# First expert phase entered by token tiles, with the next routing's setup behind it

## The chip, the core and the metric

One core of a Trainium2 chip runs the whole kernel. The metric is device time in microseconds, the median of several runs; lower is better. Engines are named as in the profile: PE (matmul), PEld (its weight loads), DVE (vector), ACT (activation), POOL (issues the indirect DMAs here), SP (issues the others).

## The reference

Local-and-global attention makes 4352 tokens (8 batches of 544) of width 512, and a router with capacity gives each token to one of eight experts, 544 tokens to each. The greedy walk in order of logits is what the routing has to reproduce; each expert is two matrix products with a ReLU.

```python
logits = x @ w_gate                      # N = 4352, E = 8, cap = 544
order = np.argsort(-flat)                # all (token, expert) pairs
for idx in order:
    tok, e = (int(idx) // E, int(idx) % E)
    if assigned[tok] >= 0 or counts[e] >= cap:
        continue
    assigned[tok] = e
    counts[e] += 1
...
for e in range(E):
    mask = assigned == e
    h = np.maximum(x[mask] @ w1[e], 0.0)   # 512 -> 1024
    out[mask] = h @ w2[e]                  # 1024 -> 512
```

## The kernel before

Attention fills roughly the first 230 us of the span, the first routing follows, and then come eight expert phases, one for each expert in the order in which the experts fill up.

**Precision.** Every product in a phase is made of three matmuls on rounded numbers: high by high, high by low, low by high. So each operand has a high part, which ACT rounds (`xh`, `w1h`, `w2h`, `hh`), and a low part, which DVE makes by subtracting (`xl`, `w1l`, `w2l`, `hl`).

**A phase** (`ffn`) has two halves on PE. In the H half, for each f (8 slices of 128 hidden units) and each half hf of the 544 tokens (272 columns, the slice q), a group of 12 matmuls (4 slices of the width, 3 products each; line 849) fills a PSUM tile `H` with three buffers. ACT writes `hh` from it, and DVE's `hl` is not issued at once: it is put into the list `fill` and issued at the end of the next group or when the planner sees a pause (`bubble`). After a short fp32 part (line 867) the Y half multiplies by w2, four token tiles of 24 matmuls each (line 877).

**Tokens** arrive as five tiles `xg` of 128, 128, 128, 128 and 32 rows, gathered by indirect DMA (`load_x`). `trans_x` transposes a tile on PE into an `H` buffer (line 724), ACT writes `xh` (line 726), DVE writes `xl`; those DVE rows carry the line of the wrapper `Queue`, 405.

**Routing** of the next expert runs beside a phase. `rt.setup` is ten DVE instructions (`r_m` to `r_oh`) that make `r_G` and `r_oh`; `search` has eight turns, each with 18 small matmuls `R` on PE (line 468) that read `r_G` and `r_oh`, a product `r_ce` on DVE, two more matmuls, then a scan and a new `r_G` on DVE; the rest of `phase` makes `widx` (addresses of the weights) and `idx` (addresses of the tokens).

**Order.** Every engine works through its instructions in the order in which this program issues them. A planner written into the kernel sets that order: `V.now` is its estimate of PE's time, `V.busy` its estimate of DVE's, booked by `Queue` as 130 ns and 1.05 or 0.55 ns for each element. After each matmul `step` adds to `V.now`, may issue one waiting item of `todo` (low parts of weights, transposes of the next phase, output), and lets the routing go on once `V.now` has passed the time that it asked for, which is `V.busy + HOP` before each group of its matmuls.

**The entry to the first phase** (lines 890 to 914) is written out by hand: first routing, gathers of x and w2, some idle matmuls (`HEAT`), the setup of the next routing, the low parts of the first halves of w1 (`split_w1`, line 702 in the trace), the transposes of all five tiles, and then `V.now = V.busy` and the phases.

Of the kernel before, what the change touches and what calls it, by code (L numbers as in the profile page):

```python
# [8 lines left out]
F32 = mybir.dt.float32  # L9
# [3 lines left out]
AF = mybir.ActivationFunctionType  # L13
ALU = mybir.AluOpType
# [4 lines left out]
B, H, SL, SG, D = 8, 8, 512, 32, 64  # L19
# [645 lines left out]
def experts(ctx, tc, A, xd, ident, rt, out):  # L665
    nc = tc.nc
    wp = ctx.enter_context(tc.tile_pool(name="wp", bufs=1))
    st = ctx.enter_context(tc.tile_pool(name="st", bufs=2))
    ps = ctx.enter_context(tc.tile_pool(name="fps", bufs=1, space=PSUM))
    w1h = [wp.tile([128, FF], F32R, name=f"w1h{c}") for c in range(4)]  # L670
    w1l = [wp.tile([128, FF], F32R, name=f"w1l{c}") for c in range(4)]
# [3 lines left out]
    xh = wp.tile([128, 4, CAP], F32R, name="xh")  # L675
    xl = wp.tile([128, 4, CAP], F32R, name="xl")
    hh = wp.tile([128, 8, CAP], F32R, name="hh")
    hl = wp.tile([128, 8, CAP], F32R, name="hl")
    h32 = wp.tile([128, 8, 32], F32, name="h32")
    part = [wp.tile([128, DM], F32R, name=f"part{k}") for k in range(2)]  # L680
    sizes = [128, 128, 128, 128, 32]
    HF = CAP // 2
# [5 lines left out]
    def load_w1(ph):  # L688
        raws = []
        for k in range(2):  # L690
            raw = st.tile([128, 2, FF], F32, name="w1r", bufs=2)
            gather(raw.rearrange("p a b -> p (a b)"), A["w1"], k * E * 128 * 2 * FF, rt.widx[ph][:, :1])
            raws.append(raw)
        return raws
# [5 lines left out]
    def split(hi, lo, raw, eng):  # L700
        nc.scalar.activation(hi, raw, AF.Copy)  # L701
        eng.tensor_tensor(lo, raw, hi, op=ALU.subtract)

    def split_w1(raws, j, eng):
        q = slice(512 * (j % 2), 512 * (j % 2) + 512)
        split(w1h[j // 2][:, q], w1l[j // 2][:, q], raws[j // 4][:, (j // 2) % 2, q], eng)
# [13 lines left out]
    def trans_x(xg, t):  # L720
        n = sizes[t]
        p = ps.tile([128, 4, 128], F32, name="H", bufs=3)
        for d in range(4):
            nc.tensor.transpose(p[:, d, :n], xg[t][:n, 128 * d:128 * d + 128], ident[:n, :n])  # L724
        q = slice(128 * t, 128 * t + n)
        nc.scalar.activation(xh[:, :, q], p[:, :, :n], AF.Copy)
        V.tensor_tensor(xl[:, :, q], p[:, :, :n], xh[:, :, q], op=ALU.subtract)
# [6 lines left out]
    V = rt.V  # L734
    V.now = V.busy = 0.0
    pool, dma, need = [0.0], [0.0], [0.0]
    fill, todo, raw1 = [], [], {}
# [20 lines left out]
    def bubble():  # L758
        while fill:
            fill.pop(0)()  # L760

    def at(tag, t, f, cond=None):
        todo.append((tag, t, cond, f))

    def pending(*tags):
        return any(x[0] in tags for x in todo)

    def force(tag, n=9):
        while pending(tag) and n:
            todo.pop([x[0] for x in todo].index(tag))[3]()  # L770
            n -= 1

    def step(ns):
        V.now += ns
        for i, (tag, t, cond, f) in enumerate(todo):
            if t <= V.now and (cond is None or cond()):
                todo.pop(i)
                f()
                break
        while not done[0] and V.now >= need[0]:  # L780
            v = next(routing, None)
            if v is None:
                done[0] = True
            elif v < 0:
                bubble()
            else:
                need[0] = v
        if V.busy < V.now and (done[0] or need[0] > V.now + SLACK):
            bubble()
# [7 lines left out]
    def get_w1(p, half):  # L797
        raw1[p] = load_w1(p)
        r = [pool_op(1040, 1 << 20) for _ in range(2)]
        for i in range(4):  # L800
            at(f"a{p}", r[i // 2], lambda j=2 * i: low1(p, j), lambda: (half or mid[0] == p - 1) and calm())
        for i in range(4):
            at(f"b{p}", r[i // 2], lambda j=2 * i + 1: low1(p, j), lambda: mid[0] == p - 1 and calm())

    def get_x(p):
        xg = load_x(p)
        for t in range(5):
            r = pool_op(1040, sizes[t] * 2048)
            at(f"x{p}", r, lambda t=t: trans_x(xg, t), lambda: mid[0] == p - 1)

    def get_w2(p):
        load_w2(p)
        r = [pool_op(1040, 1 << 20) for _ in range(2)]
        for j in range(8):
            at(f"w{p}", r[j // 4], lambda j=j: low2(j), lambda: cur[0] == p and calm())

    def out_tile(ph, t, p):
        n = sizes[t]
        while len([x for x in todo if x[0] == "out"]) > 3:
            force("out", 1)  # L820
        y = st.tile([128, DM], F32, name="y", bufs=4)
        nc.scalar.activation(y[:n], p[:n], AF.Copy)  # L822

        def put():
            scatter(ph, t, y)
            wrote[0] = pool_op(1040, n * 2048) + LAND
        at("out", V.now + 900, put, lambda: V.now >= wrote[0])

    def ffn(ph):
        nxt = ph + 1  # L830
        t0 = V.now
        cur[0] = ph
        half = []
        if nxt < E:
            at(f"g{nxt}", t0, lambda: get_w1(nxt, half), lambda: nxt in rt.widx and not pending(f"b{ph}"))
            at(f"h{nxt}", t0, lambda: get_x(nxt), lambda: nxt in rt.idx and (mid[0] == ph or V.now > t0 + TX))
            at(f"v{nxt}", t0, lambda: get_w2(nxt), lambda: mid[0] == ph and nxt in rt.widx and
               (not pending(f"h{nxt}") or V.now > t0 + TW))
        for f in range(8):
            if f == 4:  # L840
                force(f"b{ph}")
                half.append(True)
            for hf in range(2):
                q = slice(HF * hf, HF * hf + HF)
                p = ps.tile([128, HF], F32, name="H", bufs=3)
                fs = slice(128 * f, 128 * f + 128)
                for d in range(4):
                    for k, (w, x) in enumerate(((w1h, xh), (w1h, xl), (w1l, xh))):
                        nc.tensor.matmul(p, w[d][:, fs], x[:, d, q], start=(d + k == 0), stop=(d + k == 5))  # L849
                        step(117)  # L850
                nc.scalar.activation(hh[:, f, q], p, AF.Relu)  # L851
                if hf:
                    nc.scalar.activation(h32[:, f], p[:, HF - 32:HF], AF.Relu)  # L853
                while fill:
                    fill.pop(0)()
                fill.append(lambda p=p, f=f, q=q: V.scalar_tensor_tensor(
                    hl[:, f, q], p, 0.0, hh[:, f, q], op0=ALU.max, op1=ALU.subtract))

        while fill:
            fill.pop(0)()  # L860
        force(f"w{ph}")

        p = ps.tile([128, DM], F32, name="Y", bufs=3)
        for i in range(2):
            for c in range(4):
                f = 2 * c + i
                nc.tensor.matmul(p[32 * c:32 * c + 32], h32[:, f], w2r[f // 4][:, f % 4], start=(i == 0), stop=(i == 1))  # L867
            step(930)
        mid[0] = ph
        nc.scalar.activation(part[0], p, AF.Copy)  # L870
        V.tensor_tensor(part[1], p, part[0], op=ALU.subtract)
        for t in range(4):
            p = ps.tile([128, DM], F32, name="Y", bufs=3)
            for f in range(8):
                q = slice(128 * t, 128 * t + 128)
                for k, (h, w) in enumerate(((hh, w2h), (hh, w2l), (hl, w2h))):
                    nc.tensor.matmul(p, h[:, f, q], w[f], start=(f + k == 0), stop=(f + k == 9))  # L877
                    step(216)
            out_tile(ph, t, p)
            if t == 0:  # L880
                p = ps.tile([128, DM], F32, name="Y", bufs=3)
                for k in range(2):
                    nc.tensor.matmul(p[:32], rt.eye4, part[k], start=(k == 0), stop=(k == 1))
                    step(216)
                out_tile(ph, 4, p)
        while nxt < E and (pending(f"g{nxt}", f"h{nxt}", f"a{nxt}", f"x{nxt}", f"v{nxt}") or nxt not in raw1):
            step(120)
            bubble()

    raws = None  # L890
# [3 lines left out]
    for _ in rt.phase(0):  # L894
        if raws is None and 0 in rt.widx:
            raws = load_w1(0)
    xg = load_x(0)
    load_w2(0)
    for _ in range(HEAT):
        nc.tensor.matmul(heat[:, :128], ident, ident, start=True, stop=True)  # L900
    raw1[0] = raws
    for _ in rt.setup(slice(0, 34)):
        pass
    for j in range(4):
        split_w1(raws, 2 * j, nc.vector)
    for t in range(5):
        trans_x(xg, t)
    V.now = V.busy
    for j in range(4):
        at("b0", 0, lambda j=j: low1(0, 2 * j + 1), calm)  # L910
    for j in range(8):
        at("w0", 0, lambda j=j: low2(j), calm)
    for ph in range(E):
        ffn(ph)
    force("out")


# [75 lines left out]
```

## Time and profile before

| | us |
|---|---|
| median of 3 runs | 772.55 (771.23 to 774.29) |
| profiled execution | 769.7 |
| its span, first to last instruction | 767.9 |
| mean granted PE clock | 0.971 |
| PE busy in the span | 708.8 |
| DVE busy in the span | 506.8 |

Times within the profile count from the span's first instruction. A row of the timeline gives start, length, engine, line, operation, what it writes and reads, and in brackets how long the engine was idle before it and what ended that. A row of busy time by stretch gives the stretch, its length, then busy time and count of instructions for PE, PEld, DVE, ACT and POOL, the granted clock, the DMA engines' share and GB/s.

### The profile page before, as it was taken

What the parts mean: (1) busy time and instruction counts of PE and PEld (TensorE: products, weight loads), DVE (VectorE), ACT (ScalarE), POOL (GpSimd) and SP (SyncE); (2) the same over time, 40 slices, a digit from 0 to 9 for tenths busy, and PEclk for the clock granted to TensorE, in tenths of its full rate; (3) what the DMA queues carried; (4) which work ended last, traced back from release to release, by engine and by line L of the source; (5) the groups of instructions that cost most, each with busy time, mean ns of one, the idle gap of its engine ahead of it and who ended that gap; (6) DMA issues with size and microseconds to landing.
All of it is one profiled execution on the core that took longest, in us unless ns stands there. A gap on an engine that the chain in (4) does not pass through costs nothing.

```text
span 767.9 us, 21120 instructions
## 1 busy us (share of the span) xinstructions
PE 708.8 (92%) x8636; PEld 568.8 (74%) x8636; DVE 506.8 (66%) x1829; ACT 313.1 (41%) x849; POOL 162.2 (21%) x190
## 2 busy tenths in 40 slices
PE   8999999999994489999998999999998999999993
PEld 7667777777762378789688778778777877988972
DVE  6788787777786777677577667677666766641400
ACT  4656666666650143244144134224323414542310
POOL 5221111111000220240231151043024015312011
PEclk9999999999997579999999999999999999999998
DMA  9999879878501340440250081072044018531000
GB/s 353 404 359 341 329 278 332 281 300 321 195 20 56 124 154 2 180 146 13 107 202 28 9 287 43 1 256 82 1 167 156 15 38 286 175 117 59 1 32 27
DMA packets 32415, 120.50 MB, mean 157 GB/s; under 512 B 6720, under 2 KB 6976, under 8 KB 24128
## 3 DMA queue, kind: packets, MB, share of 16 engines
q1 hardware_dynamic: 22080, 67.78, 23.8%
q0 software_dynamic: 10240, 51.39, 18.9%
q8 instruction: 68, 1.11, 0.6%
q14 instruction: 27, 0.22, 0.1%
HBM read 101.32 MB, written 17.83 MB: 155 GB/s over the span
## 4 chain that ended last, share of the span: by engine, by line
PE 47%; DVE 7%; DMA 3%; issue 3%; ACT 3%; POOL 0%; POOLq 0%; ACTq 0%; DVEq 0%
PE Y L877 20%; PE H L849 18%; PE R L468 5%; DMA xg<-xd,idx 2%; PE Y L867 2%; DVE w2l L405 2%; PE H L724 2%; DVE r_G L405 1%; ACT w2h L701 1%; DMA w1r<-in_w_dram,widx 1%; DVE hl L405 1%; DVE w1l L405 1%; DVE r_pm L405 1%; ACT w1h L701 0%; DVE xl L405 0%
## 5 line engine op out<-in xcount | busy, mean ns | idle before, releaser
L849 PE MATMUL H<-xh,w1h 128*128 128x272 f32 x512 | 152.8, 298 | 12.7 <-DVE hl L405 10.7
L849 PE MATMUL H<-xh,w1l 128*128 128x272 f32 x512 | 150.6, 294 | 0.0
L849 PE MATMUL H<-xl,w1h 128*128 128x272 f32 x512 | 149.9, 293 | 0.0
L849 PEld LDWEIGHTS H<-xh,w1h 128*128 128x128 f32 x512 | 97.3, 190 | 17.8 <-DVE hl L405 8.7
L145 ACT ACTIVATE p<-p,nm 128x128 f32<-128x128 f32 x256 | 81.8, 392 | 65.8 <-DVE ls L165 33.7
L851 ACT ACTIVATE hh<-H 128x272 fp32r<-128x272 f32 x128 | 51.0, 398 | 138.6 <-PE H L849 138.4
L877 PE MATMUL Y<-w2h,hh 128*128 128x512 f32 x256 | 103.3, 403 | 0.0
L877 PE MATMUL Y<-w2h,hl 128*128 128x512 f32 x256 | 102.8, 401 | 0.0
L877 PE MATMUL Y<-w2l,hh 128*128 128x512 f32 x256 | 102.6, 401 | 0.0
L849 PEld LDWEIGHTS H<-xl,w1h 128*128 128x128 f32 x512 | 97.6, 191 | 0.0
L849 PEld LDWEIGHTS H<-xh,w1l 128*128 128x128 f32 x512 | 97.4, 190 | 0.0
L134 PE MATMUL S<-qk,qz 128*64 128x128 f32 x1024 | 70.7, 280 | 4.4 <-DVE qz L86 1.8
L685 POOL DMA_INDIRECT w1r<-in_w_dram,widx x16 | 16.2, 1013 | 268.0 <-DVE r_a L405 160.9
L822 ACT ACTIVATE y<-Y 128x512 f32<-128x512 f32 (+1 forms) x40 | 23.5, 594 | 120.8 <-PE Y L877 102.0
L405 DVE SCALAR_TENSOR_TENSOR hl<-H,hh 128x272 fp32r<-128x272 f32 x128 | 53.6, 434 | 25.9 <-ACT h L853 15.3
L86 POOL COPY qz<-q 64x544 f32<-64x544 f32 x60 | 38.7, 645 | 146.2 <-DMA q<-in_qk_dram 104.2
L134 PEld LDWEIGHTS S<-qk,qz 128*64 128x64 f32 x1024 | 55.3, 138 | 16.8 <-issue 9.7
L405 DVE TENSOR_TENSOR w2l<-w2r,w2h 128x512 fp32r<-128x512 f32 x64 | 42.7, 689 | 37.2 <-ACT w2h L701 36.7
L731 POOL DMA_INDIRECT out_dram<-y,idx x40 | 41.8, 1045 | 116.9 <-ACT y L822 57.3
L141 DVE CUSTOM_DVE_ANT_0 p<-S,mask 128x128 f32<-128x128 f32 x256 | 58.8, 285 | 6.1 <-PE S L134 4.4
L877 PEld LDWEIGHTS Y<-w2h,hh 128*128 128x128 f32 x256 | 48.2, 188 | 16.0 <-issue 5.9
L701 ACT ACTIVATE w1h<-w1r 128x512 fp32r<-128x512 f32 x64 | 36.7, 623 | 46.4 <-DMA w1r<-in_w_dram,widx 46.2
(164 smaller groups left out, 1213.7 us busy)
## 6 DMA issues: line engine op xcount, KB each, us to landing
vw<-in_vw_dram SPq DMA_DIRECT2D x32, 1040.0 KB, 7.9
qk<-in_qk_dram SPq DMA_DIRECT2D x32, 432.0 KB, 5.5
q<-in_qk_dram SPq DMA_DIRECT2D x32, 272.0 KB, 5.4
xd<-xs SPq DMA_DIRECT2D x8, 1024.0 KB, 6.4
xd<-xg SPq DMA_DIRECT2D x64, 8.0 KB, 5.2
xg<-xd,idx POOLq DMA_INDIRECT x40, 3.7
out_dram<-y,idx POOLq DMA_INDIRECT x40, 2.8
mask<-in_mask_dram SPq DMA_DIRECT2D x1, 512.0 KB, 5.5
```

What stands on the lines that cost most here:

```text
L86: eng.tensor_copy(z[r, :, h, :], q[r].rearrange("p (j i) -> p j i", i=32))
L134: nc.tensor.matmul(st[64 * r:64 * r + 64, c, :], z[:, j].rearrange("p h i -> p (h i)"), kw[:, k0:k0 + 128], start=True, stop=True)
L141: nc.vector.tensor_tensor_reduce(s.p[:, c, :], st[:, c, :], mask[:, 4 * s.u + c, :], 1.0, -BIG, ALU.add, ALU.max, nm[:, c:c + 1])
L145: nc.scalar.activation(s.p[:, c, :], s.p[:, c, :], AF.Exp, bias=nm[:, c:c + 1], scale=SCALE)
L405: return op(*args, **kw)
L468: s.nc.tensor.matmul(out, *args, **kw)
L701: nc.scalar.activation(hi, raw, AF.Copy)
L731: nc.gpsimd.indirect_dma_start(out=out, out_offset=bass.IndirectOffsetOnAxis(ap=rt.idx[ph][:n, t:t + 1], axis=0), in_=y[:n], in_offset=None)
L822: nc.scalar.activation(y[:n], p[:n], AF.Copy)
L849: nc.tensor.matmul(p, w[d][:, fs], x[:, d, q], start=(d + k == 0), stop=(d + k == 5))
L851: nc.scalar.activation(hh[:, f, q], p, AF.Relu)
L877: nc.tensor.matmul(p, h[:, f, q], w[f], start=(f + k == 0), stop=(f + k == 9))
```

## The change

At the entry, the low parts of w1 come first, then the transposes of three tiles, then the setup; in the first phase alone the groups begin with (f, hf) = (0, 0), (1, 0), and tiles 3 and 4 are transposed in front of (0, 1), which is followed by (1, 1) and the usual order. The two loops over f and hf become one; for the other phases they run as they did.

```diff
-    def ffn(ph):
+    def ffn(ph, late=None):
...
-        for f in range(8):
-            if f == 4:
+        groups = [(f, hf) for f in range(8) for hf in range(2)]
+        if late:
+            groups[:4] = (0, 0), (1, 0), (0, 1), (1, 1)
+        for f, hf in groups:
+            if (f, hf) == (4, 0):
                 force(f"b{ph}")
                 half.append(True)
-            for hf in range(2):
...
+            if (f, hf) == (0, 1) and late:
+                late()
...
     raw1[0] = raws
+    for j in range(4):
+        split_w1(raws, 2 * j, nc.vector)
+    for t in range(3):
+        trans_x(xg, t)
     for _ in rt.setup(slice(0, 34)):
         pass
-    for j in range(4):
-        split_w1(raws, 2 * j, nc.vector)
-    for t in range(5):
-        trans_x(xg, t)
     V.now = V.busy
...
     for ph in range(E):
-        ffn(ph)
+        ffn(ph, (lambda: [trans_x(xg, t) for t in (3, 4)]) if ph == 0 else None)
```

More of the change, by code (lines that the diff above doesn't have):

```diff
@@ L838, in ffn @@
                (not pending(f"h{nxt}") or V.now > t0 + TW))
-        for f in range(8):
-            if f == 4:
+        groups = [(f, hf) for f in range(8) for hf in range(2)]
[3 more added lines that the diff above has]
+            if (f, hf) == (4, 0):
                 force(f"b{ph}")
                 half.append(True)
-            for hf in range(2):
[L844 to L857, printed above, removed]
+            if (f, hf) == (0, 1) and late:
+                late()
+            q = slice(HF * hf, HF * hf + HF)
+            p = ps.tile([128, HF], F32, name="H", bufs=3)
+            fs = slice(128 * f, 128 * f + 128)
+            for d in range(4):
+                for k, (w, x) in enumerate(((w1h, xh), (w1h, xl), (w1l, xh))):
+                    nc.tensor.matmul(p, w[d][:, fs], x[:, d, q], start=(d + k == 0), stop=(d + k == 5))
+                    step(117)
+            nc.scalar.activation(hh[:, f, q], p, AF.Relu)
+            if hf:
+                nc.scalar.activation(h32[:, f], p[:, HF - 32:HF], AF.Relu)
+            while fill:
+                fill.pop(0)()
+            fill.append(lambda p=p, f=f, q=q: V.scalar_tensor_tensor(
+                hl[:, f, q], p, 0.0, hh[:, f, q], op0=ALU.max, op1=ALU.subtract))
         while fill:
```

## The prediction

> **What bounds the kernel now.** I read the page's first two parts, then the timeline around the seam between attention and the first expert phase, then busy time by half phase, then the chain and the waits at the next seams.
>
> ```profile
> PE 708.8 (92%) x8636; PEld 568.8 (74%) x8636; DVE 506.8 (66%) x1829; ACT 313.1 (41%) x849; POOL 162.2 (21%) x190
> PEclk9999999999997579999999999999999999999998
> ```
>
> PE is busy for 92% of the span, and the expert phases are one in-order PE queue: a microsecond by which PE is late there is still there at the end. The one dip of the granted clock is slices 13 to 16, the seam that the change rearranges. Its timeline:
>
> ```profile
> 265.89 0.42 DVE L405 TENSOR_REDUCE r_m<-L 128x34 f32<-128x272 f32 x1
> 267.08 1.15 ACT L701 ACTIVATE w1h<-w1r 128x512 fp32r<-128x512 f32 x2 [2.05 <-DMA w1r<-in_w_dram,widx]
> 268.57 0.44 DVE L405 TENSOR_TENSOR r_oh<-r_v,r_mo 128x272 bf16<-128x272 bf16 x1
> 269.04 2.50 DVE L702 TENSOR_TENSOR w1l<-w1r,w1h 128x512 fp32r<-128x512 f32 x4
> 272.31 0.63 PE L724 MATMUL H<-ident,xg 128*128 128x128 f32 x4 [0.80 <-DMA xg<-xd,idx]
> 272.98 0.60 ACT L726 ACTIVATE xh<-H 128x512 fp32r<-128x512 f32 x1 [0.84 <-PE H L724]
> 273.61 0.69 DVE L405 TENSOR_TENSOR xl<-H,xh 128x512 fp32r<-128x512 f32 x1 [0.74 <-ACT xh L726]
> 273.87 1.65 PE L724 MATMUL H<-ident,xg 128*128 128x128 f32 x8 [0.93 <-DMA xg<-xd,idx]
> 275.45 0.59 PE L849 MATMUL H<-xh,w1h 128*128 128x272 f32 x1
> 275.63 0.89 DVE L405 TENSOR_TENSOR xl<-H,xh 128x512 fp32r<-128x512 f32 x2 [1.33 <-ACT xh L726]
> 275.85 0.43 PE L849 MATMUL H<-xl,w1h 128*128 128x272 f32 x1
> 277.88 0.43 PE L849 MATMUL H<-xl,w1h 128*128 128x272 f32 x1
> 278.24 0.30 PE L468 MATMUL R<-r_oh,r_G 128*32 128x16 bf16 x17
> 278.53 0.57 PE L849 MATMUL H<-xh,w1l 128*128 128x272 f32 x1
> 278.90 0.43 PE L849 MATMUL H<-xh,w1h 128*128 128x272 f32 x1
> 280.00 0.29 PE L849 MATMUL H<-xh,w1l 128*128 128x272 f32 x1
> 280.88 0.29 PE L849 MATMUL H<-xh,w1h 128*128 128x272 f32 x1
> 281.11 0.37 PE L849 MATMUL H<-xl,w1h 128*128 128x272 f32 x1
> ```
>
> The routing's setup runs on DVE from 265.89 to 269.01 (3.12 us), while PE and ACT wait for x; then the four low parts of w1; then xl. Tile 2 (third row of L724) is set by its DMA, not by DVE: its xl waits for ACT's xh. The last two tiles' transposes and the first H matmul follow each other on PE without a gap. I number the H matmuls: 1 starts at 275.45, 2 at 275.85, 11 at 277.88, 12 at 278.53, 13 at 278.90, 18 at 280.00, 25 at 280.88, 26 at 281.11; a group is 12. From 2 to 11 the step is 2.03/9 = 0.226 us, from 18 to 25 0.88/7 = 0.126: the clock was at half until about 279.8:
>
> ```profile
> 266.50:269.50 3.00, 2.98 (x14) 2.68 (x14) 2.90 (x10) 1.15 (x2) 2.37 (x3) 0.50 0.43 109
> 269.50:270.00 0.50, 0.50 (x4) 0.38 (x3) 0.50 (x2) 0.00 (x0) 0.22 (x1) 0.80 0.83 320
> 270.00:273.00 3.00, 1.41 (x10) 0.84 (x8) 2.83 (x5) 1.22 (x3) 2.39 (x3) 1.00 0.60 183
> 273.00:273.50 0.50, 0.00 (x0) 0.00 (x0) 0.00 (x0) 0.50 (x1) 0.50 (x1) 0.62 0.41 131
> 273.50:276.50 3.00, 2.63 (x12) 2.27 (x13) 1.57 (x4) 1.58 (x5) 1.04 (x2) 0.50 0.69 228
> 276.50:279.50 3.00, 3.00 (x30) 2.73 (x30) 2.50 (x7) 1.26 (x4) 0.00 (x0) 0.50 0.96 391
> 279.50:280.00 0.50, 0.50 (x5) 0.50 (x3) 0.00 (x0) 0.50 (x2) 0.00 (x0) 0.55 0.78 328
> ```
>
> Each row is a stretch, its length, busy time of PE, PEld, DVE, ACT, POOL, then the clock. From the mean clock of the three half-microsecond rows it rose at about 269.7 (0.80), fell at 273.1 (0.62) and rose at 279.8 (0.55). It was whole only after a stretch with PE busy throughout (2.98 of 3.00), and half again after one at 1.41; the stretch at 2.63 of 3.00 did not raise it.
>
> **The change, part by part.** (a) Low parts of w1 and xl ahead of setup. w1l can start at 265.96 where setup started, its third waits for ACT (267.08 row), all are done near 269; and xl of tile 0 follows its xh at once. No gain on the path: tile 2's xl still waits for its DMA, transposes and xh, and ends at 274.30. POOL's ten gathers and the ACT halves of w1 do not depend on setup and keep their places; SP has nothing here. I cost (a) at 0.
>
> (b) H enters on three tiles. Group (0,0) takes columns 0 to 271, which are tiles 0, 1 and 16 columns of 2. Matmul 1 can start when xh of tile 2 is there (273.58), matmul 2 with its xl (274.30, so 274.33): 1.52 earlier than 275.85. At 0.226, matmul 11 is at 276.36, and its successor would go at 276.6.
>
> (c) Setup after that. On DVE its ten instructions are now queued behind xl of tile 2, so they run from 274.30 to 277.42. The planner still puts the first R matmuls after matmul 11 (V.now and V.busy start equal, and the first two events are the same), and R reads r_G and r_oh: PE waits from 276.6 to 277.45. Matmul 12 then comes 0.29 and 13 0.66 after R, as in the rows: 13 at 278.11, 0.79 earlier than before. The lead has halved. With the clock raised at 279.8, seven and a half more matmuls at 0.226 and four and a half at 0.126 bring group (1,0) to its end at 280.4, where before had reached 280.88: a lead of 0.5.
>
> (d) Tiles 3 and 4, now between groups. All of (0,1) reads tiles 2 to 4, and PE has nothing else queued. The nearest rows are the same eight transposes at the next seam:
>
> ```profile
> 335.59 0.96 PE L724 MATMUL H<-ident,xg 128*128 128x128 f32 x8
> 336.23 0.60 ACT L726 ACTIVATE xh<-H 128x512 fp32r<-128x512 f32 x1 [1.00 <-PE H L724]
> 336.86 0.95 DVE L405 TENSOR_TENSOR xl<-H,xh 128x512 fp32r<-128x512 f32 x2 [0.33 <-ACT xh L726]
> ```
>
> From the transposes' start to the end of both xl, 337.81 - 335.59 = 2.2 us. There other H matmuls cover it; here nothing does. ACT's hh of (1,0) is just done when xh is due, and DVE has worked off its three w1l. So matmul 26 starts at 280.4 + 2.2 + 0.05 = 282.65 against 281.11: 1.5 to 1.6 us late. The PSUM slot costs nothing more: hl of (1,0) is not yet issued, so (0,1) can only take the slot that xl of tile 3 or 4 frees, and it waits for xl anyway. I take +1.6. Bounds: without the wait in (c) +1.0; with the clock one stretch later (below) +2.4, two stretches later +3.7.
>
> (e) The planner. xl of tiles 3 and 4 (130 + 512 x 1.05 and 130 + 128 x 1.05, by Queue: 932 ns) used to be booked before V.now = V.busy; now they are booked inside the phase, and every turn of the search waits for V.busy + 400. I carried those bookings through the phase, for order alone: before gives R after matmul 11, its second part after 25, and three, then five Y matmuls ahead of the last transposes, as the trace has it. After: the second turn comes after matmul 54 instead of 46, and idx of phase 1 after the phase's matmul 262 instead of 258: four Y matmuls later (4 x 216 = 864 of the 932). That is the place it has in phase 1 of before, so the Y half of phase 0 becomes like that of phase 1, and phase 1 starts in the order of phases 2 to 5. What these orders cost is in the rows:
>
> ```profile
> 305.74:336.48 30.74, 30.74 (x214) 23.26 (x213) 21.12 (x65) 8.63 (x17) 10.77 (x12) 1.00 0.52 184
> 365.66:397.49 31.83, 31.58 (x215) 23.00 (x215) 20.80 (x64) 9.38 (x18) 11.68 (x11) 1.00 0.49 178
> 428.67:460.49 31.82, 31.58 (x215) 23.00 (x215) 20.81 (x64) 9.38 (x18) 11.68 (x11) 1.00 0.52 178
> 336.48:365.66 29.18, 28.32 (x312) 26.38 (x311) 22.14 (x51) 12.78 (x35) 3.36 (x3) 1.00 0.08 29
> 397.49:428.67 31.18, 28.83 (x311) 26.48 (x311) 22.48 (x52) 12.15 (x34) 3.00 (x3) 1.00 0.07 27
> 460.49:491.61 31.12, 28.79 (x311) 26.45 (x311) 22.44 (x52) 12.14 (x34) 2.95 (x3) 1.00 0.07 27
> ```
>
> ```profile
> 336.55 1.72 PE H L849 x12
> 397.49 1.65 PE H L849 x11
> ```
>
> ```profile
> PE H L849 <- DVE hl L405: 0.9, 2, 0.6
> PE H L849 <- DVE hl L405: 2.4, 4, 0.8
> ```
>
> First fence, busy time by stretch: Y halves of phases 0, 1, 2, then H halves of phases 1, 2, 3. Second: the chain's first H pieces of phases 1 and 2 (the first R comes after 12 matmuls or after 11). Third: PE's waits in those two H halves: with R one matmul earlier, hl falls behind scan and G on DVE four times instead of twice. Phases 2 and 3 repeat to 0.1 us, so order sets this. Y half of phase 0: 31.83 - 30.74 = +1.1 (the later tiles' DMA wait is inside it, since phase 1 has idx as close to its end). H half of phase 1: 31.18 - 29.18 = +2.0. From there both kernels have the same order. Bounds: 0 for each if real waits hide the shift, these values otherwise. In the rest of phase 0's H half the new order leaves 15 or more matmuls (1.9 us) between a scan and the group that needs its hl: no new stall counted, up to 0.3.
>
> **The sum.** 1.6 + 1.1 + 2.0 = +4.7 us. The profiled execution took 769.7 (span 767.9), so 774.4 for such a one; the median of the runs shown is 772.55, 2.85 above the profiled one, so 777.3.
>
> **Rivals.** *The clock rises later* (+0.8, 778.1; two stretches +2.1, 779.4). The new wait of (c) lies in the stretch 276.5 to 279.8 that raised the clock before: PE is then busy for some 2.5 of 3.3 us, near the row with 2.63 that did not raise it. Against: half of that row was transposes, not H. With half clock the group ends at 280.8 and the trip is 276.52 - 273.87 = 2.65 (cold rows above), so matmul 26 is at 283.5. The Trainium skill, TensorE: Matmul & The Clock Gate, Part 1, says that the clock rises after about 3.4 us of sustained work, judged in a free-running window; Part 4 there says that transposes do not count as such work. By the first sentence the gap delays the rise and this rival holds; by the second the row with 2.63 tells nothing against the window, and the forecast holds. The trace's rises and falls lie 3.4 us and 6.7 us apart, which agrees with such a window, and it does not separate the two readings.
>
> *Only the entry counts* (774.2, within 0.5%): the planner's shift changes the order but the later halves do not lengthen. For it: nothing on PE reads idx until the seam. Against: phases 2 and 3, with one order, agree to 0.1, and phase 1, with another, does not.
>
> *The lead is kept* (not slower, 771.5): if PE could go on while setup and the tile trip run, the start is 1.1 earlier. It decides at one place: R after matmul 11 not waiting for r_oh, and (0,1) not for xl. Against: DVE runs in order, and (0,1) needs tiles 3 and 4 at once. Should the order instead fall on that of phase 1 in all later phases, four H halves would save 2.0 each (about 768): the bookings do not give it.
>
> **How the numbers follow.** Forecast 0.48 (775.5 to 778.3), later clock 0.22, only the entry 0.15, lead kept 0.11, better order later 0.04. The point is the forecast's. The range goes from 773.0, below the entry's lower bound of +1.0, to 780.0, above the clock's two stretches: 0.82 of the chance. A run of this kernel tells 0.5% (3.9 us) from nothing: forecast mostly beyond that, later clock all: slower 0.60; within 0.36; faster 0.04.
>
> **What would show it.** First H matmul near 273.7 and a gap until 274.3; R near 277.4 with PE waiting for r_oh; a PE gap of about 1.3 us before (0,1), ended by xl; the last H matmul of phase 0 some 1.6 later than before; phase 0's Y half near 31.8; phase 1's H half near 31.2 with four hl waits and R after 11. Wrong if R does not wait, if (0,1) starts at once, or if phase 1 stays at 29.2.

## The result: 780.5 us against 773.4, slower by 1%

| kernel | median, us | before in the same comparison | ratio (95% interval) |
|---|---|---|---|
| the change | 780.46 | 773.36 | 1.0101 (1.0061 to 1.0141) |
| the change, a second time | 779.38 | 773.7 | 1.0068 (1.0043 to 1.0092) |

The forecast was 777.3, 4.7 above the kernel before; measured were 7.1 and 5.7 more than before. Every run is in the fast state but one of the order alone below (785.35), which is left out of its median. The profiled execution of the changed kernel took 779.72 (span 777.9, against 769.7 and 767.9). Two lines of its page, engine totals and the clock in 40 slices:

```profile
PE 712.1 (92%) x8636; PEld 569.1 (73%) x8636; DVE 506.3 (65%) x1829; ACT 313.1 (40%) x849; POOL 161.3 (21%) x190
PEclk9999999999996589999999999999999999999997
```

The work is the same (8636 matmuls, DVE 506) and PE is busy for only 3.3 us more. Of the 10.0 us by which the span grew, two thirds are time in which PE does nothing. The dip of the clock fills the same three slices (6 5 8 for 7 5 7), though H begins earlier. Rows of the timeline of the entry:

```profile
273.60 0.59 PE L853 MATMUL H<-xh,w1h 128*128 128x272 f32 x1 [0.69 <-issue]
274.19 0.43 DVE L405 TENSOR_REDUCE r_m<-L 128x34 f32<-128x272 f32 x1
274.33 0.60 PE L853 MATMUL H<-xl,w1h 128*128 128x272 f32 x1
276.54 0.43 PE L853 MATMUL H<-xl,w1h 128*128 128x272 f32 x1
276.89 0.44 DVE L405 TENSOR_TENSOR r_oh<-r_v,r_mo 128x272 bf16<-128x272 bf16 x1
277.39 0.29 PE L468 MATMUL R<-r_oh,r_G 128*32 128x16 bf16 x17 [0.42 <-DVE r_oh L405]
278.02 0.43 PE L853 MATMUL H<-xh,w1h 128*128 128x272 f32 x1
280.35 0.29 PE L853 MATMUL H<-xh,w1l 128*128 128x272 f32 x1
280.48 0.96 PE L724 MATMUL H<-ident,xg 128*128 128x128 f32 x8
281.74 0.89 DVE L405 TENSOR_TENSOR xl<-H,xh 128x512 fp32r<-128x512 f32 x2 [1.01 <-ACT xh L726]
282.58 0.36 PE L853 MATMUL H<-xh,w1h 128*128 128x272 f32 x1 [1.14 <-DVE xl L405]
282.88 0.37 PE L853 MATMUL H<-xl,w1h 128*128 128x272 f32 x1
```

Matmul 1 at 273.60 and 2 at 274.33; setup on DVE from 274.19; R at 277.39 after a wait for r_oh; matmul 13 at 278.02; the last matmul of group (1,0) is the row at 280.35; then come the trip of tiles 3 and 4, matmul 25 at 282.58, and matmul 26 at 282.88, where before had 281.11: 1.77 late (1.6 forecast). The planner's part, as busy time by stretch: Y half of phase 0, H half of phase 1, then Y and H halves of phases 1 and 2:

```profile
308.60:341.18 32.58, 31.58 (x216) 22.94 (x215) 20.89 (x64) 9.39 (x18) 11.00 (x12) 1.00 0.50 174
341.18:372.33 31.15, 28.82 (x310) 26.48 (x311) 22.45 (x52) 12.19 (x34) 2.96 (x3) 1.00 0.08 27
372.33:404.21 31.88, 31.60 (x215) 23.00 (x214) 20.82 (x64) 9.38 (x18) 11.68 (x11) 1.00 0.50 177
404.21:435.46 31.25, 28.79 (x310) 26.45 (x310) 22.39 (x52) 12.14 (x34) 2.93 (x3) 1.00 0.07 27
```

Phase 1's H half is 31.15, 1.97 longer than before's 29.18 (2.0 forecast); phase 0's Y half 32.58, 1.84 longer (1.1 forecast). PE's waits, first from matmul 25 to the end of phase 0's H half (the wait for xl is that of matmul 25, the trip itself), then in phase 1's (the wait for xl is that of its first matmul, and lies in the Y half before it). The line ahead of them is the same part of phase 0 in the kernel before, from matmul 26 on:

```profile
PE H L849 <- DVE hl L405: 0.2, 1, 0.2
...
PE H L853 <- DVE xl L405: 1.1, 1, 1.1
PE H L853 <- DVE hl L405: 0.9, 2, 0.6
...
PE H L853 <- DVE hl L405: 2.3, 4, 0.8
PE H L853 <- DVE xl L405: 1.0, 1, 1.0
```

That two hl waits of 0.9 stand in phase 0 where before had one of 0.2 was not forecast. From matmul 26 to matmul 192, the last of the half, before takes 305.53 - 281.11 = 24.42 and the change 308.38 - 282.88 = 25.50: +1.08. Rows of the longer of the two waits, and then of the same turn's scan in the kernel before, where an hl went ahead of it:

```profile
288.93 1.29 DVE L405 TENSOR_TENSOR w2l<-w2r,w2h 128x512 fp32r<-128x512 f32 x2 [0.34 <-ACT w2h L701]
290.14 0.42 DVE L405 TENSOR_TENSOR_SCAN r_pm<-R,fin 128x128 f32<-128x128 f32 x1
290.60 0.79 DVE L405 SCALAR_TENSOR_TENSOR r_G<-r_x,r_pm,cf 128x544 bf16<-128x544 f32 x1
291.30 0.78 DVE L405 SCALAR_TENSOR_TENSOR hl<-H,hh 128x272 fp32r<-128x272 f32 x2
291.79 0.39 PE L853 MATMUL H<-xh,w1h 128*128 128x272 f32 x1 [0.65 <-DVE hl L405]
...
286.35 0.43 DVE L405 SCALAR_TENSOR_TENSOR hl<-H,hh 128x272 fp32r<-128x272 f32 x1
286.70 0.41 DVE L405 TENSOR_TENSOR_SCAN r_pm<-R,fin 128x128 f32<-128x128 f32 x1
```

In the change two hl stand in DVE's queue behind scan and r_G, and these behind two w2l that had waited for ACT. PE needs the H buffer that the first hl frees. The Trainium skill, TensorE: Matmul & The Clock Gate, Part 1, says that VectorE's queue is strictly first in, first out; these rows agree.

The four pieces add up to 1.77 + 1.08 + 1.84 + 1.97 = 6.7 in this pair of profiles. The rest of the 10.0 lies in later phases, above all 5 and 6, in pieces that also differ between executions of one kernel: the H half of phase 6 is 27.92 in one execution of before and 29.76 in another, and 30.06 in this one of the change (see the last section).

### The profile page after: what moved, and what is told of

It reads as the page before. It is cut to its first block, busy times and chain, and to the rows that moved or that the text cites. A ratio compares the mean times of both kernels' runs of the same rounds, so it can differ in the third digit from the quotient of the medians.

```text
span 777.9 us, 21121 instructions
## 1 busy us (share of the span) xinstructions
PE 712.1 (92%) x8636; PEld 569.1 (73%) x8636; DVE 506.3 (65%) x1829; ACT 313.1 (40%) x849; POOL 161.3 (21%) x190
## 4 chain that ended last, share of the span: by engine, by line
PE 72%; DVE 14%; issue 5%; ACT 4%; DMA 3%; another core or an unknown queue 0%; POOL 0%; POOLq 0%; ACTq 0%; DVEq 0%
PE Y L881 19%; PE H L853 17%; PE S L134 8%; PE R L468 5%; PE T L150 4%; PE O L162 4%; DVE r_G L405 3%; DVE w2l L405 2%; PE S L195 2%; DMA w1r<-in_w_dram,widx 2%; PE T L259 2%; PE Y L871 2%; PE O L234 2%; PE T L224 2%; DVE r_pm L405 1%
```

## The experiments

Theory A: entry and order each cost what the four pieces say, independently of each other. Rivals: B, the loss is all in the entry, and later halves only shift; C, the early entry is worth something that a wait or the bad order hides. Each run has its own comparison with the kernel before; "H half" and "Y half" are times between first matmuls in its profile.

**Both kernels again**, unchanged.

> The kernel before, unchanged, for a second trace of it: which of its waits repeat. Theory (entry and order): H half of phase 1 again 29.2 us, of phases 2 to 5 31.1 to 31.2, Y half of phase 0 30.7; the waits for xg's DMA at the last two seams (1.16 and 0.38) vary from run to run. Rival (chance waits): the half phases differ by over 0.5 us from the first trace. Time within 0.3% of before by both.

> The changed kernel, unchanged, for a second trace. Theory (entry and order): matmul 26 again 1.8 us later than before against the span, first H half +2.9 us, phase 0's Y half +1.1 to +1.8, phase 1's H half +2.0; ACT's wait of 2.8 us in phase 6 and the 1.5 us for xg ahead of it are gone or elsewhere. Rival (they belong to the change): the same waits at the same places. Time 779 to 782.

773.17 against 773.7, 0.9985 (0.9964 to 1.0007), and 779.38, 1.0068. Three of the four pieces repeat: from matmul 26 to 192 24.43 and 25.51, Y half of phase 0 31.00 and 32.56, H half of phase 1 29.32 and 31.26. The entry moves: the first gather of x to matmul 26 takes 15.08 and 14.37 us in the two profiles of before, 16.81 and 17.97 in those of the change.

**The order alone**: the kernel before, with 932 ns booked after 24 matmuls of phase 0.

```diff
+                if (ph, f, hf) == (0, 1, 0):
+                    V.busy += 932
```

> The kernel before with one line more: after matmul 24 of phase 0 the planner's V.busy is raised by 932 ns, so that from there PE's order of R and H is that of the changed kernel; the entry stays as it was. Theory (order counts): the rest of phase 0's H half +1.1 us, its Y half +1.1, phase 1's H half +2.0, together +3.1 to +5.0 (776.5 to 778.5). Rival (only the entry counts): 0 to +0.5 us (773 to 774).

776.98 against 773.7, 1.004 (1.001 to 1.007): +3.3 with the entry untouched. In its profile the turns of R stand behind the same matmuls as in the change, in phases 0, 1 and 2 (in phase 0 behind 11, 54, 91, 124, 157 and 186). Its waits between matmul 26 and the end of phase 0's H half, and its Y half of phase 0:

```profile
PE H L851 <- DVE hl L405: 0.9, 2, 0.6
```

```profile
307.35:339.94 32.59, 31.64 (x215) 23.00 (x214) 20.89 (x64) 9.38 (x18) 11.01 (x12) 1.00 0.48 173
```

The same two hl waits, 25.48 from matmul 26 to 192, 32.59, and 31.14 for the H half of phase 1: three of the four pieces come from one booked number, with the same instructions in another order. In this profile they add up to 4.9, which the interval (+0.8 to +5.4) includes. B falls.

**The entry alone**: the change, with xl of tiles 3 and 4 issued past the planner.

```diff
-    def trans_x(xg, t):
+    def trans_x(xg, t, eng=None):
...
-        V.tensor_tensor(xl[:, :, q], p[:, :, :n], xh[:, :, q], op=ALU.subtract)
+        (eng or V).tensor_tensor(xl[:, :, q], p[:, :, :n], xh[:, :, q], op=ALU.subtract)
...
-        ffn(ph, (lambda: [trans_x(xg, t) for t in (3, 4)]) if ph == 0 else None)
+        ffn(ph, (lambda: [trans_x(xg, t, nc.vector) for t in (3, 4)]) if ph == 0 else None)
```

> The changed kernel, but with xl of tiles 3 and 4 issued past the planner, so that its bookings and PE's order after matmul 24 are those of before. Theory (entry and order): only the entry's +1.6 to +1.8 us is left (775 to 775.5), phase 0's Y half back at 30.7, phase 1's H half at 29.2. Rival (only the entry counts): as slow as the changed kernel, 779 to 781.

774.95 against 773.7, 1.0023 (0.9995 to 1.005): +1.3, not distinguishable from zero. Matmul 26 to 192 is back at 24.57, Y half of phase 0 30.98, H half of phase 1 29.16. The entry costs 17.21 to matmul 26.

**R one matmul earlier in phase 1 alone**, and **one later in phases 2 to 5**, both in the kernel before:

```diff
+        if ph == 1:
+            need[0] -= 120
```

> The kernel before, with the time at which the planner lets the routing go on pulled 120 ns ahead at the start of phase 1 alone: the first R comes after 11 H matmuls instead of 12, and the rest of that phase's order is that of phases 2 to 5. Theory (order counts): phase 1's H half 31.15 us instead of 29.2, the other halves unchanged, time +2.0 (about 775.5). Rival (phase 1 is short for another reason, such as what is in flight at its start): 29.2 and 0.

```diff
+        if 2 <= ph < 6:
+            need[0] += 100
```

> The opposite: the kernel before, with that time pushed 100 ns back at the start of phases 2 to 5, so that all of them have phase 1's order, R after 12. Theory (order counts): four H halves at 29.2 instead of 31.15, -7.8 us (about 765.5 to 766). Rival (phase 1 is short for another reason): within 0.5 us of before.

The first: 773.22 against 770.17, 1.0029 (1.0006 to 1.0051), +3.1 (2.0 expected, inside the interval); H half of phase 1 31.14 and the other H halves as before. The second: 764.18 against 770.17, 0.9909 (0.9882 to 0.9935), 6.0 faster than before (about 7.8 expected). Its H halves of phases 1, 2 and 3, and its waits in phase 2's:

```profile
338.82:368.02 29.20, 28.32 (x313) 26.37 (x311) 22.20 (x51) 12.78 (x35) 2.18 (x3) 1.00 0.08 29
399.85:429.01 29.16, 28.29 (x310) 26.36 (x310) 22.46 (x52) 12.15 (x34) 2.94 (x3) 1.00 0.08 29
460.84:490.05 29.21, 28.34 (x312) 26.40 (x311) 22.42 (x52) 12.28 (x34) 3.49 (x3) 1.00 0.08 29
```

```profile
PE H L851 <- DVE hl L405: 0.9, 2, 0.6
```

So the place of R within a half phase, one matmul of 0.126 us, is worth 2.0 us in each H half, either way.

**The entry without its waits.** First the setup ahead of all else again (R then finds r_oh), beside the unbooked xl; then also all f < 4 of the first token half ahead of tiles 3 and 4, with their transposes in other PSUM buffers, so that H matmuls cover the trip.

```diff
+    for _ in rt.setup(slice(0, 34)):
+        pass
     for j in range(4):
         split_w1(raws, 2 * j, nc.vector)
     for t in range(3):
         trans_x(xg, t)
-    for _ in rt.setup(slice(0, 34)):
-        pass
```

> The changed kernel with the bookings of before (xl of tiles 3 and 4 past the planner) and with the setup back ahead of w1l and the tiles: takes away PE's wait for r_oh and leaves the wait for tiles 3 and 4. Theory: R no longer waits, matmul 12 follows 11; of the entry's loss 0.6 us goes, +1.0 to +1.2 is left (774.5). Rival (the wait for setup only uncovers another wait there): as e2_unbooked, +1.3 to +1.8.

```diff
-        p = ps.tile([128, 4, 128], F32, name="H", bufs=3)
+        p = ps.tile([128, 4, 128], F32, name="Y" if eng else "H", bufs=3)
...
-            groups[:4] = (0, 0), (1, 0), (0, 1), (1, 1)
+            groups[:8] = [(f, hf) for hf in range(2) for f in range(4)]
...
-            if (f, hf) == (0, 1) and late:
+            if (f, hf) == (2, 0) and late:
```

> As e6_setup_first, and groups (2,0) and (3,0) go between the transposes of tiles 3 and 4 and group (0,1); the two transposes use the PSUM tiles of the Y half, so that H keeps its three. It takes away both waits of the entry. Theory: no PE gap ahead of matmul 25, matmul 26 within 0.3 us of before against the gathers, time -0.3 to +0.3 (about 773.5). Rival (starting H on three tiles is a gain once nothing waits): -1.0 to -1.5.

772.39 and 770.73 against 770.17: 1.0023 (1.001 to 1.0036) and 1.0007 (0.9991 to 1.0023). The first is 2.2 slower than before, where 1.0 to 1.2 was expected: the removed wait for r_oh shows no gain in time, though in the profile matmul 26 comes 15.32 after the first gather and no longer 17.21. In the second, with both waits gone, the start on three tiles is worth nothing that can be measured; in no run was it worth something. C falls for this kernel. Matmul 26 comes 15.32 and 15.15 after the first gather, no earlier than with the old entry (14.04 to 15.25): H begins 1.6 to 2.1 us earlier after the gather and runs longer at half clock (3.9 and 5.4 us, against 1.9 to 4.5 with the old entry).

**The change with R one matmul later in phases 1 to 5**, and **the covered entry with the later R**:

```diff
+        if 1 <= ph < 6:
+            need[0] += 100
```

> The changed kernel with the routing's first turn in the later phases one matmul later (100 ns more on the planner's time asked for, in phases 1 to 5). If an H half's length is set by the routing's place alone, five H halves fall from 31.2 to 29.2 us, 10 us less than the changed kernel: about 770, 0.4% under the kernel before, although entry, first H half and first Y half stay as bad as they are (start of matmul 26 some 17 us after the first gather, 25.5 us from there to matmul 192, a Y half of 32.6). If the changed kernel's loss were in the entry or in something that hangs on it through all phases, it stays above the kernel before.

> The entry on three tiles with its two new waits removed (setup first, tiles 3 and 4 transposed under the groups of the first half of the tokens), the late subtractions not booked, and the turn after 12 matmuls in phases 2 to 5. If entry and order add up as independent terms, this comes out at the kernel with the turn after 12 alone, 764, within 2 us: the early entry gains nothing even with cover, and four H halves save 7. If the early entry was worth something that a bad later order hid, it is below 762.

767.24 against 769.64, 0.9964 (0.9941 to 0.9987), and 764.25 against 769.64, 0.9934 (0.9903 to 0.9964). The first was expected 0.4% under the kernel before and is 0.36% under it; the second lands where the later R alone landed (764.18), so the terms add and the early entry adds nothing. The first's H halves are 29.20 and its entry is as bad as the change's (17.27 to matmul 26). Its Y half of phase 0, which is issued in the change's own order, is 31.84 and not 32.58:

```profile
311.68:343.52 31.84, 31.65 (x216) 23.01 (x215) 20.99 (x64) 9.39 (x18) 10.69 (x11) 1.00 0.50 178
```

**hl ahead of scan**: the search gives way once more, so that a waiting hl is issued before it; with the later R in the kernel before, and by itself in the change.

```diff
             yield -1
             yield s.V.ready()
+            yield -1
             for k in range(2):
```

> The kernel before with the turn after 12 matmuls in all phases, and the search made to give way once more between its r_ce product and its scan, so that a waiting hl can be issued ahead of the scan. In the H halves of the kernel with the turn after 12 there are still two waits of PE for hl, 0.9 us a phase. If these come from hl standing behind scan and r_G in DVE's queue, they go and each H half falls below 29.2 towards 28.3: about 4 to 5 us off the 764.2 of the turn after 12 alone. Rival: hl is late for another cause (ACT's hh or the low part of w2 ahead of it), or the routing falls behind and the wait moves into the fp32 part or the Y half: 764 or more.

> The changed kernel, with the one edit that lets a waiting hl go ahead of the routing's scan; the planner's times stay as the change has them. If the 1.07 us between matmul 26 and 192 of the first phase and the 2 us of the second phase's H half are hl standing behind scan and r_G, both go: first H half from matmul 26 to 192 24.4 us or less, H halves of phases 1 to 5 at 27.7 to 29.2 us where they were 31.2, so 11 to 18 us off the changed kernel. What then stays against the kernel before with the same edit and R after 12 (755.1) is the entry (1.7 to 2.8) and the Y half of the first phase (1.1 to 1.8): 757 to 760. Rival: hl is late through ACT or the low part of w2 there; then the two waits of the first phase stay, and the time is above 762.

755.08 against 769.64, 0.98 (0.9759 to 0.984): 14.6 faster than the kernel before, the best version here. In the change: 760.41 against 773.13, 0.9841 (0.9774 to 0.9907). DVE in phase 2 of the kernel before, then the same scan in the first of the two (where R also comes one matmul later), and the H halves of its phases 1 and 2:

```profile
401.89 0.42 DVE L405 TENSOR_TENSOR_SCAN r_pm<-R,fin 128x128 f32<-128x128 f32 x1
402.34 0.79 DVE L405 SCALAR_TENSOR_TENSOR r_G<-r_hi,r_pm,cf 128x544 bf16<-128x544 int32 x1
403.05 0.78 DVE L405 SCALAR_TENSOR_TENSOR hl<-H,hh 128x272 fp32r<-128x272 f32 x2
403.53 0.39 PE L849 MATMUL H<-xh,w1h 128*128 128x272 f32 x1 [0.64 <-DVE hl L405]
```

```profile
401.76 0.43 DVE L405 SCALAR_TENSOR_TENSOR hl<-H,hh 128x272 fp32r<-128x272 f32 x1
402.11 0.41 DVE L405 TENSOR_TENSOR_SCAN r_pm<-R,fin 128x128 f32<-128x128 f32 x1
402.56 0.79 DVE L405 SCALAR_TENSOR_TENSOR r_G<-r_hi,r_pm,cf 128x544 bf16<-128x544 int32 x1
403.26 0.43 DVE L405 SCALAR_TENSOR_TENSOR hl<-H,hh 128x272 fp32r<-128x272 f32 x1
```

```profile
338.21:365.94 27.73, 27.73 (x312) 26.25 (x310) 21.86 (x51) 12.78 (x35) 3.36 (x3) 1.00 0.08 31
397.79:425.56 27.77, 27.77 (x311) 26.28 (x311) 22.15 (x52) 12.16 (x34) 3.61 (x3) 1.00 0.08 30
```

In the first fence both hl come after r_G and PE waits 0.64; in the second one goes ahead of scan, and no matmul of the half waits: PE is busy for 27.73 of 27.73. I had expected 28.3 as the floor. The gain over the later R alone is 14.6 - 6.0 = 8.6 us, each against its own comparison, and 5 x 1.45 + 0.5 = 7.7 by the halves; 4 to 5 had been expected. In the change, the edit removes the hl waits of both H halves. The rows are the H half of phase 0 from matmul 26 to its end (to the first fp32 matmul; 25.72 in the change), the Y half, and the H half of phase 1:

```profile
284.12:308.13 24.01, 24.01 (x268) 22.75 (x266) 18.30 (x42) 9.93 (x28) 0.00 (x0) 1.00 0.01 2
308.13:340.86 32.73, 31.70 (x216) 22.95 (x215) 20.94 (x64) 9.38 (x18) 11.12 (x12) 1.00 0.47 173
340.86:368.62 27.76, 27.76 (x311) 26.25 (x311) 22.25 (x52) 12.19 (x34) 2.95 (x3) 1.00 0.08 31
```

No gap is left in either H half, although R's turns keep their places to within two matmuls (the first two exactly); the Y half between them keeps its 32.73. So the +1.08 and the +2.0 are one mechanism, an H buffer held by an hl behind scan and r_G. The low parts of the weights, which wait for ACT, still stand ahead of the hl there and no longer make PE wait; whether moving them instead would have done as much was not tried. What is still lost against the best version is the entry (16.75 to matmul 26 against 15.25), that Y half (32.73 against 30.74) and, in these two profiles, phase 6 (29.65 against 27.78), which varies between executions: together 5.4 in the profiles. The medians lie 5.3 apart, but the kernel before, too, was 3.5 higher in the second comparison (773.13 against 769.64); each against its own, the two versions are 14.6 and 12.7 faster, only 1.8 apart, so the times do not confirm that sum. I had expected 757 to 760.

## Why the prediction was right or wrong

The direction and the sequence of steps held; the size was short by 1.0 to 2.4 us. Of the 3.2 us by which 777.3 missed 780.46, 0.8 is the starting point (772.55, where the comparison has 773.36 for the kernel before) and 2.4 the difference. By the steps:

- **(a)** Costed at 0: nothing on the path was gained by it. Matmul 1 followed tile 2's xh at once, as forecast.
- **(b), (c)** Forecast 274.33, 277.45, 278.11 and 280.4 for matmul 2, R, matmul 13 and the end of group (1,0); measured 274.33, 277.39, 278.02 and 280.48.
- **(d)** Forecast +1.6 at matmul 26, measured +1.77 between the first two profiles. The trip took 2.15, from 280.48 to the end of xl at 282.63 (2.2 forecast). But "the PSUM slot costs nothing more" was not quite so: matmul 25, which reads no xl, waited for xl all the same, since it needs an H buffer, and two R matmuls follow it, so matmul 26 came 0.25 after xl and not 0.05. Over all profiles the term was too small. From the first gather to matmul 26, six profiles with the old entry take 14.04 to 15.25 (mean 14.64), five with the new one 16.75 to 17.97 (mean 17.20): +2.6. Partly this is the rival *clock rises later*. The rows in which it rose, in the profile of the change and in its repeat:

```profile
279.50:280.00 0.50, 0.50 (x4) 0.50 (x3) 0.50 (x2) 0.00 (x0) 0.00 (x0) 0.50 0.25 98
280.00:280.50 0.50, 0.50 (x6) 0.50 (x5) 0.50 (x2) 0.00 (x0) 0.00 (x0) 0.87 0.00 0
```

```profile
281.00:281.50 0.50, 0.50 (x4) 0.50 (x3) 0.06 (x1) 0.18 (x1) 0.00 (x0) 0.50 0.04 16
281.50:282.00 0.50, 0.50 (x5) 0.33 (x4) 0.00 (x0) 0.23 (x2) 0.00 (x0) 0.87 0.00 0
```

  From the mean clocks it rose at 280.13 and 281.63, 14.1 and 15.8 after the first gather. All five profiles with the new entry: 13.2 to 15.8, mean 14.55; the six with the old: 11.3 to 14.1, mean 12.78. By estimate, 1.8 us more at half clock, 0.226 for 0.126 a matmul, cost 1.8 x (1 - 0.126/0.226) = 0.8. The profile of before that I worked from had risen at 13.92 (at 279.95 by its row's 0.55, where the prediction reads 279.8), late among its own kind, so its entry showed little of what was to be lost. The clock's own record adds this: in all fourteen profiles the stretches of one granted clock around the seam last whole multiples of 3.41 us (in before 3.41 from 269.70 and 6.83 from 273.12), and where these steps fall against the gather differs from execution to execution. The step that holds the wait for r_oh, in the change and in its repeat:

```profile
276.71:280.13 3.42, 3.00 (x31) 2.82 (x30) 3.35 (x10) 0.92 (x2) 0.00 (x0) 0.50 0.87 364
274.80:278.21 3.41, 2.99 (x29) 2.75 (x30) 3.31 (x12) 0.65 (x2) 0.00 (x0) 0.50 0.93 377
```

  The clock rose at the end of the first and not at the end of the second, with PE busy for 3.00 and 2.99 us; in the repeat it rose one step later, after PE had been busy throughout. The wait is the only idle time in either step (0.42), so a step that holds it stands at the edge: it can delay the rise by 3.41 us, and does not always. The prediction left open whether transposes count for the rise; in this case they do. In the profile with R one matmul earlier in phase 1 the step that ended in the rise is the following, all of PE and then the transposes alone, 1.55 of the 3.42 us:

```profile
277.58:281.00 3.42, 3.42 (x16) 3.02 (x17) 2.21 (x5) 2.39 (x5) 0.89 (x1) 0.50 0.83 302
277.58:281.00 3.42, 1.55 (x8) 1.08 (x8) 0.50 0.83 302
```

  So the reading by which the row with 2.63 tells nothing against the window, on which the forecast rested, does not hold here. In the three runs that keep the early entry without the wait for r_oh, the clock rose at 11.4, 13.2 and 13.9, which overlaps both groups. The Trainium skill, TensorE: Matmul & The Clock Gate, Part 1, calls the window free-running and the number of cold matmuls variable from run to run; the spread within one kernel agrees. My 0.48 against 0.22 for it was too sure from one profile.
- **(e), H half of phase 1** Forecast +2.0, measured +1.97, by four hl waits (2.3 us) instead of two. R after 11 in it and in phases 2 to 5, as carried through.
- **(e), rest of phase 0's H half** The failed step, a term put at nothing: "15 or more matmuls (1.9 us) between a scan and the group that needs its hl: no new stall counted, up to 0.3". It cost 1.07, in every run with that order and hl behind scan (25.50, 25.51, 25.48 and 25.52) and in none without. The count of matmuls was right, 16 and 15 ahead of the two waits; that they cover the time was not. DVE does not begin the scan when R is done, since w2l, waiting for ACT's w2h, stands ahead of it: in the rows above it begins at 290.14, where R's last matmul had ended at 289.07, and scan, r_G and hl take 1.6 from there. That they are in hl's way is shown by the run that put hl ahead of them; the part of w2l is read from the rows alone.
- **(e), Y half of phase 0** Forecast +1.1 from phase 1's 31.83. One run with the new order has it (31.84); four have 32.56 to 32.73. In two of those ACT's xh of tile 2 starts 0.7 late; in the other two PE waits 0.4 and 0.5 for the first tile's DMA. Why is open: the order issued is the same. A late xh of tile 2 occurs with the old order as well (the repeat of before, the unbooked xl), where that half is only 0.25 longer, 31.00 and 30.98.

With means over the runs, 2.6 + 1.1 + 1.5 + 2.0 = 7.2, beside the 7.1 and 5.7 measured and the 4.7 forecast: the failed step is 1.1 of the shortfall, the entry 1.0, the Y half 0.4. The rival *only the entry counts* is refuted by the order alone (+3.3), *the lead is kept* by every run. The remark that four H halves would save 2.0 each under phase 1's order held for the halves where it was tried (1.9 to 2.0 each); in time it was 6.0 for 8.

## What to carry to other kernels

An instruction order made by an estimate can turn on one small booking: 932 ns booked in another place moved the routing's turns, in the second phase by a single matmul, and cost 3.3 us, so after an edit, carry the planner's numbers through to the order before costing the edit itself. When counting whether a result comes in time on an in-order engine, count from when the engine gets to it, with all that stands ahead and what that waits for, not from where it is issued. And an earlier start of matrix work is not yet a gain: here 1.5 us of lead were 0.4 after two groups and a loss of 1.8 after the next dependence, and with both waits removed the earlier matmuls ran at half clock and nothing was gained.

## What was unexpected

One operation's place in DVE's queue was worth more than anything tuned around it: hl ahead of scan and R one matmul later take 14.6 us (2%) off, and leave the H halves of phases 1 to 5 with PE busy throughout. And ACT once stands still for over 2 us for what the profile puts down to a remote event, in three of fourteen profiles, at hh in all three (2.8, 2.8 and 2.3 us). It occurs with and without the change and was not explained. These are the three profiles whose H half of phase 6 lasts 29.65 to 30.06; in the other eleven it lasts 27.78 to 28.65. The row of the changed kernel's waits:

```profile
ACT hh L855 <- remote: 2.8, 1, 2.8
```
